# Attention and feed-forward on one core: one token layout for all pairs, per-chunk decay with the state on VectorE, and a new first block

## The chip, the cores and the metric

The kernel runs on one core of one Trainium2 chip. The metric is the device time of one execution in microseconds (us). A run is marked slow when it is over 1.5% above the fastest run of the same kernel. A "ratio" below is the recorded one of a kernel's fast runs to the fast runs of the kernel before on the same chip, with a 95% interval. It comes close to the ratio of their means, but is not exactly that, nor the ratio of the medians that stand beside it. The medians are those of all runs, slow ones too.

Engines: PE is TensorE (matmuls), PEld its weight loads, DVE is VectorE, ACT is ScalarE, POOL is GpSimd, SP is SyncE (which here only issues DMAs). "L357" is line 357 of the kernel of that run; the same statement has other line numbers in other kernels. "The Trainium skill" is a collection of notes on the chip; its pages are named by their titles.

## The reference

A linear recurrence with a decay per token (4 batches, 8 heads, 768 tokens, head size 32, state size 16), followed by a gated feed-forward layer on all 3072 tokens.

```python
# per batch and head; a in [0.85, 0.95], chunks of 32 tokens in the reference
for c in range(nc):
    cum = cumsum(log_a[chunk])
    L = exp(cum[:, None] - cum[None, :]) * causal
    y = (C @ B.T * L) @ x                         # inside the chunk
    y += (C @ state) * exp(cum)[:, None]          # from the chunks before
    state = exp(sum(log_a)) * state + sum_j exp(cum[-1] - cum[j]) * B[j] x[j]
# then, on x = y as (3072, 256), with 1536 hidden columns:
out = (maximum(x @ w_gate, 0) * (x @ w_val)) @ w_out
```

Both kernels use chunks of 128 tokens, in bf16 on TensorE. A *pair* is two chunks (256 tokens), a *block* two pairs (512 tokens); there are 12 pairs in 6 blocks. In block b, the attention of the next block's pairs P and Q is threaded between the feed-forward matmuls of block b.

## The kernel before

Pairs 0 to 3 are loaded two tokens per partition, so that a DMA packet can hold two tokens of a head instead of one. TensorE then sorts them into token order with a 0/1 matrix. Later pairs are loaded in token order.

```python
    def sort_wide(p, engs=None, own=False):
        ...
        for i in range(2):
            ...
            for r in range(2):
                nc.tensor.matmul(out=o[:, 0:128], lhsT=order[:, i, r], rhs=s["tin"][0][r], ...)
                nc.tensor.matmul(out=o[:, 128:384]..., lhsT=order[:, i, r], rhs=s["xw"][:, r], ...)
            (eng.copy if eng is nc.scalar else eng.tensor_copy)(out=bx[:, i], in_=o)
```

The decay is a running product over half a sequence. So the state needs no decay between chunks, and it grows in one PSUM bank, A_ps. VectorE only reads it through a mask.

```python
    def astep(p, i):                       # one 128x256 matmul a chunk
        nc.tensor.matmul(out=A_ps, lhsT=st[p]["B"][i], rhs=st[p]["x"][i],
                         start=(c == 0), stop=(c == NC - 2), ...)
    def sevac(p, i):                       # Sm: the state, spread for the next chunk's matmul
        nc.vector.tensor_tensor(out=n, in0=A_ps, in1=smask, op=ALU.mult)
```

The other steps of a pair: `G` computes the scores of four groups of heads into four banks, `gevac` copies them out through the causal mask (masked scores `gs`), `inter` multiplies the earlier state with C, `Dm` multiplies `gs` with x (the *masked product*), `yevac` has ScalarE move the result to `yT`, the input of the feed-forward. `gvh` and `gv` are gate and value matmuls on 256 or 512 tokens, with a relu on ScalarE and a product `h` on VectorE; `fout` is the output matmul. In the code and in the recorded texts, f counts the twelve columns of weights of 128 hidden units each. A *filler*, or warm-up matmul, is one whose result nobody uses; it only keeps TensorE busy. Five PSUM banks are shared by all steps. In the chains shown below each engine takes up its instructions in the order of the program, also where a later one could have started sooner.

```python
        if more:                            # end of a block
            inter(P, 0); inter(P, 1)
        fout(b, 0); foevac(b, 0)
        if more:
            G(P); gevac(P)
        fout(b, 1); foevac(b, 1)
        if more and b > 0:
            state(Q, 0)
        fout(b, 2); foevac(b, 2)
        if more:
            Dm(P); yevac(P, nc.scalar)
            G(Q); gevac(Q)
            state(Q, 1 if b else 0)         # behind Q's masks
        fout(b, 3); foevac(b, 3)
```

Of the kernel before, what the change touches and what calls it, by code (L numbers as in the profile page):

```python
# [29 lines left out]
def kernel(  # L30
# [18 lines left out]
    BH = NB * NH  # L49
# [5 lines left out]
    NBLK = T // 512  # L55

    const = ctx.enter_context(tc.tile_pool(name="const", bufs=1))
    glob = ctx.enter_context(tc.tile_pool(name="glob", bufs=1))
    raw = ctx.enter_context(tc.tile_pool(name="raw", bufs=4))
# [8 lines left out]




    NWIDE = 4
    st = {}

    def wide_bc(p, qb, qc):
        b, c0 = p // PPB, 2 * (p % PPB)
        sl = slice(c0 * 128, (c0 + 2) * 128)
        bcr = raw.tile([128, NH, 2, 2, N], FP32, tag="bcr", name="bcr")
        for src, j, q in ((C, 1, qc), (B, 0, qb)):
            if (p, j) in ((0, 0), (2, 1)):  # L80
                nc.vector.memset(bcr[0:1, 0, 0, 0, 0:1], 0.0)  # L81
            q.dma_start(
                out=bcr[:, :, j].rearrange("p h r n -> p h (r n)"),
                in_=src[b, :, sl, :].rearrange("h (p r) n -> p h (r n)", r=2))
        st.setdefault(p, {})["bcr"] = bcr

    def wide_x(p, *qs):

        b, c0 = p // PPB, 2 * (p % PPB)
        sl = slice(c0 * 128, (c0 + 2) * 128)  # L90
        xr = raw.tile([128, NH, 2, D], FP32, tag="xr", name="xr")
        n = NH // len(qs)
        for k, q in enumerate(qs):
            hs = slice(k * n, (k + 1) * n)
            q.dma_start(out=xr[:, hs].rearrange("p h r d -> p h (r d)"),
                        in_=x[b, hs, sl, :].rearrange("h (p r) d -> p h (r d)", r=2))
        st.setdefault(p, {})["xr"] = xr

    def load(p, qx, qb, qc):
        b, c0 = p // PPB, 2 * (p % PPB)  # L100
        if p < NWIDE:
            wide_bc(p, qb, qc)
            wide_x(p, qx)
        else:
            xr = raw.tile([128, 2, NH, D], FP32, tag="xr", name="xr")
            bcr = raw.tile([128, 2, 2, NH, N], FP32, tag="bcr", name="bcr")
            for i in range(2):
                sl = slice((c0 + i) * 128, (c0 + i + 1) * 128)
                qx.dma_start(out=xr[:, i], in_=x[b, :, sl, :].rearrange("h s d -> s h d"))
                for src, j, q in ((B, 0, qb), (C, 1, qc)):  # L110
                    q.dma_start(out=bcr[:, i, j],
                                in_=src[b, :, sl, :].rearrange("h s n -> s h n"))
            st[p] = {"xr": xr, "bcr": bcr}

    H = S // 2
    HC = NC // 2
    a_sb = glob.tile([2 * BH, H], FP32)
    nc.sync.dma_start(out=a_sb, in_=a.rearrange("b h (w s) -> (b h w) s", w=2))
    first = const.tile([1, 2], FP32)
    nc.vector.memset(first, 0.0)  # L120
    nc.scalar.activation(first[:, 1:2], first[:, 0:1], AF.Relu)


    warm = const.tile([128, 512], BF16)
    nc.vector.memset(warm, 0.0)
    wide_bc(0, nc.scalar, nc.sync)
    wide_x(0, nc.sync, nc.scalar)
    wide_bc(1, nc.scalar, nc.sync)
    wide_x(1, nc.sync)
    identf = const.tile([2 * BH, 2 * BH], FP32)  # L130
# [3 lines left out]
    maskUT = const.tile([128, 1, 128], BF16)  # L134
    make_upper_triangular(nc, maskUT[:, 0], 1.0, diag=True)
    zero1 = const.tile([2 * BH, 1], FP32)
# [3 lines left out]
    bd = const.tile([128, 128], BF16)  # L140
    nc.vector.memset(bd, 0.0)
    smask = const.tile([128, 2, 128], BF16)
    for k in range(4):
        nc.vector.memset(bd[32 * k:32 * k + 32, 32 * k:32 * k + 32], 1.0)
        nc.vector.memset(tmask[32 * k:32 * k + N, 0:1], 1.0)
    nc.vector.tensor_scalar(out=tmask[:, 1:2], in0=tmask[:, 0:1], scalar1=-1.0,
                            scalar2=1.0, op0=ALU.mult, op1=ALU.add)
    for t in range(2):
        nc.vector.tensor_scalar_mul(smask[:, t], bd, tmask[:, t:t + 1])
    pick = const.tile([2 * BH, 2, BH], FP32)  # L150
    pairs = identf.rearrange("p (h w) -> p w h", w=2)
    nc.vector.tensor_copy(pick[:, 1], pairs[:, 1])
    order = const.tile([128, 2, 2, 128], BF16)
    nc.gpsimd.memset(order, 0.0)
    for r in range(2):
        nc.gpsimd.tensor_copy(
            order[:, :, r].rearrange("p c (m r) -> p c m r", r=2)[:, :, :, r],
            ident.rearrange("p (c m) -> p c m", c=2))

    def keep_warm(n):  # L160
        w = bank("w")
        for _ in range(n):
            nc.tensor.matmul(out=w, lhsT=warm[:, 0:128], rhs=warm, start=True, stop=True)  # L163

    keep_warm(8)


# [15 lines left out]
    gate = const.tile([1, 4], FP32)  # L183

    def wait_for(p, j):

        nc.gpsimd.tensor_copy(gate[:, 2 * j:2 * j + 1], st[p]["bcr"][0:1, 0, j, 0, 0:1])

    wait_for(0, 1)
    weights(0, 4)  # L190


    cp = glob.tile([2 * BH, H], FP32)
    nc.vector.tensor_tensor_scan(
        out=cp, data0=a_sb, data1=zero1.to_broadcast([2 * BH, H]), initial=1.0,
        op0=ALU.mult, op1=ALU.add)
    rmid = const.tile([2 * BH, 1], FP32)
    nc.vector.reciprocal(rmid, cp[:, H - 1:H])
    nc.vector.tensor_scalar_mul(pick[:, 0], pairs[:, 0], rmid)

    def wide_decay(ps):

        d = bank("wdec", (128, len(ps), 2, 8))
        first = True
        for k, p in enumerate(ps):
            b, c0 = p // PPB, 2 * (p % PPB)
            for i in range(2):
                w, o = (c0 + i) // HC, ((c0 + i) % HC) * 128
                for r in range(2):
                    nc.tensor.matmul(  # L210
                        out=d[64 * i:64 * i + 64, k, r],
                        lhsT=cp[:, o + r:o + 128:2], rhs=pick[:, w, 8 * b:8 * b + 8],
                        start=first or (k == 0 and r == 0), stop=True,
                        tile_position=(0, 64 * i), skip_group_check=True)
                first = False
        return d

    def wide_factors(ps, d):
        f = const.tile([128, len(ps), 2, 2, 8], FP32, name="wf%d" % ps[0])
        nc.vector.reciprocal(f[:, :, 0], d)  # L220
        nc.vector.tensor_copy(f[:, :, 1], d)
        for k, p in enumerate(ps):
            st[p]["f"] = f[:, k].rearrange("p j r h -> p (j r) h")

    scaleBC = glob.tile([128, NB, NC, 2, 8], FP32)

    def decay():

        d = bank("dec", (128, HC, 2, NB, 8))
        for k in range(HC):  # L230
            nc.tensor.matmul(
                out=d[:, k].rearrange("p w b h -> p (w b h)"),
                lhsT=cp[:, k * 128:(k + 1) * 128],
                rhs=pick.rearrange("p w h -> p (w h)"),
                start=(k == 0), stop=True, skip_group_check=True)
        for w in range(2):
            cs = slice(w * HC, (w + 1) * HC)
            nc.vector.reciprocal(
                scaleBC[:, :, cs, 0, :].rearrange("p b k h -> p k b h"), d[:, :, w])
        for w in range(2):  # L240
            cs = slice(w * HC, (w + 1) * HC)
            nc.scalar.copy(
                out=scaleBC[:, :, cs, 1, :].rearrange("p b k h -> p k b h"), in_=d[:, :, w])

    yT = glob.tile([128, 2, T], BF16)
    A_ps = mm.tile([128, 2, 128], FP32, tag="Aps", name="A_ps")


    def scale(p, eng, ceng):
        scale_bc(p, eng)  # L250
        cast_x(p, ceng)

    def scale_bc(p, eng):
        b, c0 = p // PPB, 2 * (p % PPB)
        s = st[p]
        bs = att.tile([128, 4, 128], BF16, tag="bs", name="bs")
        if p < NWIDE:
            src = s["bcr"].rearrange("s (t q) j r n -> s (j r) t q n", t=2)
            f = s["f"]
        else:  # L260
            src = s["bcr"].rearrange("s i j (t q) n -> s (i j) t q n", t=2)
            f = scaleBC[:, b, c0:c0 + 2].rearrange("s c j h -> s (c j) h")
        for t in range(2):
            eng.tensor_tensor(  # L264
                out=bs.rearrange("s k (q t n) -> s k t q n", q=4, t=2)[:, :, t],
                in0=src[:, :, t],
                in1=f[:, :, 4 * t:4 * t + 4].to_broadcast([128, 4, 4, N]),
                op=ALU.mult)
        if p < NWIDE:
            s["tin"] = [[bs[:, 2 * j + r] for r in range(2)] for j in range(2)]  # L270
        else:
            s["tin"] = [[bs[:, 2 * i + j] for i in range(2)] for j in range(2)]
            s["B"] = s["tin"][0]
# [33 lines left out]
    def transp(p, k, apart=False):  # L307

        s = st[p]
        if "tp" not in s:  # L310
            s["tp"] = {}
# [81 lines left out]
    def astep(p, i):  # L393

        c = 2 * (p % PPB) + i
        if c == NC - 1:
            return
# [260 lines left out]
```

## Time and profile before

The median was 133.82 us. The profiled execution has a span of 132.1 us.

| what | before |
|---|---|
| first gate/value matmul | 13.56 us |
| first output matmul of block 0 | 30.44 us |
| first output matmul of block 1 | 49.84 us |
| blocks 1 to 4, from one first output matmul to the next | 18.65, 18.62, 18.51, 17.62 us |
| from block 5's first output matmul to the end | 8.8 us |

These marks are the starts of the output matmuls on the timeline of PE, where block 0's is:

```profile
30.44 1.47 PE L490 MATMUL o<-wo,h 128*128 128x256 bf16 x12
```

They cut the span at places where both kernels have done the same amount of feed-forward work, so they tell where a difference arises. (The granted-clock records start at 10.57 us at full speed in this trace, and the mean granted clock leaves out what lies before; there the warm-up matmuls of 512 columns stand 0.427 us apart, which is half speed: gate/value matmuls of 512 columns stand 0.22 us apart later.)

The page of the kernel before; in the groups the columns are line, engine, operation, output and inputs, count, then total busy us, mean ns of one, and the idle time before them with what ended it:

```profile
span 132.1 us, 3133 instructions
...
PE 125.6 (95%) x1150; PEld 83.3 (63%) x1157; DVE 90.1 (68%) x196; ACT 81.7 (62%) x177; POOL 37.6 (29%) x76
...
PEclk9999999999999999999999999999999999999999
...
PE 58%; DVE 1%; issue 0%; DVEq 0%
...
L406 DVE TENSOR_TENSOR Sm<-A_ps,smask 128x256 bf16<-128x256 f32 x20 | 8.3, 417 | 0.0
```

PE is busy 95% of the span, and in the chain of work that ended last nothing but PE counts. The other engines have room. Sm takes 417 ns.

The windows view of the kernel before, cut at the first output matmuls of blocks 1 to 5, of which one block and the sum of all four are shown (busy us of each engine, instructions in brackets, granted clock, DMA share):

```profile
core 0: us, PE busy (x) PEld busy (x) DVE busy (x) ACT busy (x) POOL busy (x), PEclk, DMA share, GB/s
...
68.49:87.11 18.62, 18.57 (x181) 12.67 (x180) 13.69 (x28) 13.04 (x29) 5.43 (x10) 1.00 0.56 85
...
sum 73.40, PE 73.11 PEld 49.76 DVE 53.28 ACT 50.31 POOL 18.29; mean PE 18.28 PEld 12.44 DVE 13.32 ACT 12.58 POOL 4.57
```

In four blocks PE is idle for only 73.40 − 73.11 = 0.29 us.

The chain of the kernel before around the two masked products of one block (start, us, what):

```profile
73.24 0.34 PE y L435 x16
73.57 0.33 PE g L361 x8
73.90 0.21 PE A_ps L398
74.12 1.31 PE o L490 x12
75.43 0.87 PE gv L478 x8
76.30 0.22 PE y L424 x4
76.52 0.34 PE y L435 x16
```

From the first masked product (L435) to the second, 3.28 us pass, all of it PE's work.

### The profile page before, as it was taken

The numbers are of one execution on the slowest core, as the hardware profiler recorded it, in microseconds if no ns is written. First come the engines' busy times: TensorE is split into PE (matmuls) and PEld (weight loads), VectorE is DVE, ScalarE is ACT, GpSimd is POOL, SyncE is SP. The second block draws the span as 40 slices with busy tenths as digits, with TensorE's granted clock in tenths as the row PEclk, the third lists the DMA queues.
The fourth block names the chain that finished last, engine by engine and source line by source line (L and its number), as shares of the span: only waits on it lengthen the run. The fifth ranks groups of instructions, "written<-read, shape, count | busy, mean of one in ns | idle before, by whom it ended". The sixth has DMA issues, their size and how long they took to land.

```text
span 132.1 us, 3133 instructions
## 1 busy us (share of the span) xinstructions
PE 125.6 (95%) x1150; PEld 83.3 (63%) x1157; DVE 90.1 (68%) x196; ACT 81.7 (62%) x177; POOL 37.6 (29%) x76
## 2 busy tenths in 40 slices
PE   6999979999999999999999999999999999999990
PEld 2455655547887457786557785467875577854770
DVE  5648867786478877569977568755879775687511
ACT  4046855393579784488774588744896935876410
POOL 7327374310266000293003390003750022100000
PEclk9999999999999999999999999999999999999999
DMA  3997999996877894239970279761110002200022
GB/s 73 189 183 111 181 210 194 183 144 83 108 136 141 95 118 47 87 86 122 106 83 5 79 137 116 90 64 58 52 57 0 0 0 84 79 0 0 5 88 71
DMA packets 68995, 12.10 MB, mean 92 GB/s; under 512 B 62772, under 2 KB 68980, under 8 KB 68980
## 3 DMA queue, kind: packets, MB, share of 16 engines
q1 hardware_dynamic: 62896, 8.88, 43.7%
q0 software_dynamic: 3184, 2.36, 11.9%
q10 hardware_dynamic: 2896, 0.66, 2.7%
q8 instruction: 9, 0.15, 0.5%
q14 instruction: 10, 0.05, 0.1%
HBM read 11.11 MB, written 3.15 MB: 108 GB/s over the span
## 4 chain that ended last, share of the span: by engine, by line
PE 58%; DVE 1%; issue 0%; DVEq 0%
PE o L490 20%; PE val L463 11%; PE gv L478 11%; PE gate L460 10%; PE y L435 2%; PE g L361 2%; PE A_ps L398 1%; PE tp L318 1%; PE y L424 1%; DVE h L467 0%; DVE ob L503 0%; DVEq L503 0%
## 5 line engine op out<-in xcount | busy, mean ns | idle before, releaser
L467 DVE TENSOR_TENSOR h<-r,val 128x512 bf16<-128x512 bf16 x48 | 32.6, 686 | 9.7 <-ACT r L466 8.8
L490 PE MATMUL o<-wo,h 128*128 128x256 bf16 x288 | 35.0, 273 | 0.1
L466 ACT ACTIVATE r<-gate 128x512 bf16<-128x512 f32 x48 | 28.3, 601 | 8.5 <-PE gate L460 6.2
L369 POOL TENSOR_SCALAR_AFFINE_SELECT gs<-gs 128x512 bf16<-128x512 bf16 (+1 forms) x24 | 12.2, 530 | 65.9 <-ACT gs L380 65.9
L490 PEld LDWEIGHTS <-h 128*128 128x128 bf16 x288 | 27.4, 98 | 5.1 <-issue 1.3
L463 PE MATMUL val<-yT,wv 128*128 128x512 bf16 x96 | 28.6, 379 | 0.3
L460 PE MATMUL gate<-yT,wg 128*128 128x512 bf16 x90 | 27.3, 379 | 0.3 <-ACT r L466 0.3
L482 DVE TENSOR_TENSOR h<-r,gv 128x256 bf16<-128x256 bf16 x48 | 19.9, 421 | 7.3 <-ACT r L481 6.9
L386 DVE TENSOR_TENSOR gs<-g,maskUT 128x512 bf16<-128x512 f32 x24 | 15.5, 686 | 13.0 <-issue 11.8
L481 ACT ACTIVATE r<-gv 128x256 bf16<-128x256 f32 x48 | 18.5, 385 | 2.5 <-PE gv L478 0.9
L478 PE MATMUL gv<-yT,wg 128*128 128x256 bf16 x96 | 18.4, 273 | 0.6 <-ACT yT L448 0.5
L478 PE MATMUL gv<-yT,wv 128*128 128x256 bf16 x96 | 18.3, 273 | 0.0
L463 PEld LDWEIGHTS <-wv 128*128 128x128 bf16 x96 | 9.4, 98 | 11.3
L460 PEld LDWEIGHTS <-wg 128*128 128x128 bf16 x96 | 8.8, 98 | 7.1 <-issue 0.5
L380 ACT CAST gs<-g 128x512 bf16<-128x512 f32 x12 | 7.1, 588 | 9.7 <-PE g L361 9.6
L448 ACT CAST yT<-y 128x512 bf16<-128x512 f32 x12 | 7.0, 586 | 8.2 <-PE y L435 7.1
L478 PEld LDWEIGHTS <-wg 128*128 128x128 bf16 x96 | 9.0, 98 | 2.4 <-issue 1.0
L478 PEld LDWEIGHTS <-wv 128*128 128x128 bf16 x96 | 9.4, 98 | 1.1
L264 POOL TENSOR_TENSOR bs<-bcr,scaleBC 128x256 bf16<-128x256 f32 x16 | 9.6, 623 | 0.0
L506 ACT COPY ob<-o 128x512 f32<-128x512 f32 x10 | 5.9, 586 | 4.7 <-PE o L490 4.7
L163 PE MATMUL w<-warm 128*128 128x512 bf16 x18 | 7.3, 556 | 1.3 <-DVE bcr L81 1.3
L406 DVE TENSOR_TENSOR Sm<-A_ps,smask 128x256 bf16<-128x256 f32 x20 | 8.3, 417 | 0.0
(75 smaller groups left out, 113.1 us busy)
## 6 DMA issues: line engine op xcount, KB each, us to landing
out_dram<-ob SPq DMA_DIRECT2D x10, 256.0 KB, 2.2
xr<-in_x_dram SPq DMA_DIRECT2D x17, 128.0 KB, 3.7
bcr<-in_B_dram SPq DMA_DIRECT2D x16, 64.0 KB, 3.6
bcr<-in_C_dram SPq DMA_DIRECT2D x16, 64.0 KB, 3.3
xr<-in_x_dram SPq DMA_DIRECT2D x3, 256.0 KB, 6.4
wg<-in_moe_w_gate_dram POOLq DMA_DIRECT2D x3, 256.0 KB, 5.0
wv<-in_moe_w_val_dram POOLq DMA_DIRECT2D x3, 256.0 KB, 6.2
wo<-in_moe_w_out_dram POOLq DMA_DIRECT2D x1, 768.0 KB, 11.3
```

The source lines that it names most:

```text
L264: eng.tensor_tensor(out=bs.rearrange("s k (q t n) -> s k t q n", q=4, t=2)[:, :, t], in0=src[:, :, t], in1=f[:, :, 4 * t:4 * t + 4].to_bro ...
L369: nc.gpsimd.affine_select(out=dst, in_=dst, pattern=[[0, n], [1, 128]], compare_op=ALU.is_ge, fill=0.0, base=0, channel_multiplier=-1)
L386: nc.vector.tensor_tensor(out=d[:, q], in0=g[q], in1=m, op=ALU.mult)
L406: nc.vector.tensor_tensor(out=n, in0=A_ps, in1=smask, op=ALU.mult)
L460: nc.tensor.matmul(out=g, lhsT=wg[:, k, fs], rhs=yT[:, k, tk], start=(k == 0), stop=(k == 1))
L463: nc.tensor.matmul(out=v, lhsT=wv[:, k, fs], rhs=yT[:, k, tk], start=(k == 0), stop=(k == 1))
L466: nc.scalar.activation(r, g, AF.Relu)
L467: nc.vector.tensor_tensor(out=fst[b][:, f], in0=r, in1=v, op=ALU.mult)
L478: nc.tensor.matmul(out=gv_[:, j], lhsT=w[:, k, fs], rhs=yT[:, k, tk], start=(k == 0), stop=(k == 1), skip_group_check=True)
L481: nc.scalar.activation(r, gv_[:, 0], AF.Relu)
L482: nc.vector.tensor_tensor(out=fst[b][:, f, u * 256:(u + 1) * 256], in0=r, in1=gv_[:, 1], op=ALU.mult)
L490: nc.tensor.matmul(out=o[:, ts % 2], lhsT=fst[b][:, f, ts * 128:(ts + 1) * 128], rhs=wo[:, f], start=(f == 0), stop=(f == NF - 1), skip_gr ...
```

## The change

The intent is to drop the sorting. All pairs are loaded two tokens per partition and used in that order. The partition of a token then no longer tells its chunk by itself: partitions 0 to 63 hold chunk 0, 64 to 127 chunk 1, with even and odd tokens side by side. So matmuls over tokens are split into tiles of 64 rows, and the mask changes. The decay is now a running product per chunk of 128 tokens. The state therefore has to be multiplied by the chunk's decay, and VectorE does that in fp32, from sums that TensorE puts into a corner of the y banks. Block 0 is written out anew. The diff, cut to its core:

```diff
-        if p < NWIDE:                       # pairs 0 to 3 wide and sorted, the others in order
-    def sort_wide(p, engs=None, own=False): ...
+    def load(p):                            # all pairs: (p r) -> p, r = 2 tokens a partition
...
-        nc.tensor.matmul(out=A_ps, lhsT=st[p]["B"][i], rhs=st[p]["x"][i], ...)
+    def adds(p, at):                        # 16 matmuls of 64x32 tiles, 64 columns
+        for r in range(2):
+            for i in range(2):
+                for q in range(4):
+                    nc.tensor.matmul(out=s["A"][i][32 * q:32 * q + 32], ...
+                        tile_position=(64 * i, 32 * q), skip_group_check=True)
...
-        nc.vector.tensor_tensor(out=n, in0=A_ps, in1=smask, op=ALU.mult)
+    def state(p):
+        for i in range(2):
+            nc.vector.scalar_tensor_tensor(out=n, in0=last["S"], scalar=decay..., in1=A, ...)
+            nc.vector.tensor_tensor(out=m, in0=n..., in1=decm..., op=ALU.mult)   # Sm
...
     def Dm(p):                              # 32 matmuls of 64x32 tiles, was 16 of 128x32
...
+    def col(p, nxt=None):
+        inter(p); Dm(p)
+        if nxt is not None: adds(nxt, p)
+        yevac(p, A_)
+        if nxt is not None: state(nxt)
...
             # end of a block
-            Dm(P); yevac(P, nc.scalar)
-            G(Q); gevac(Q)
-            state(Q, 1 if b else 0)
+            col(P, Q)                       # Q's state now ahead of Q's masks
+            G(Q); gevac(Q, (P_, V, V, V))   # one mask on POOL, three on VectorE
...
+    # block 0, before the loop
+    for f in range(4): gvh(0, f, 0)
+    pair1_a()                               # scale, cast, transpose pair 1
+    gvh(0, 4, 0); gvh(0, 5, 0)
+    pair_g(1)                               # scores, adds, masks, state of pair 1
+    gvh(0, 6, 0); gvh(0, 7, 0)
+    col(1)
+    for f in range(8): gvh(0, f, 1)
+    scan(1); factors(1); decays(1)          # decay of batches 2 and 3
...
-            nc.tensor.matmul(out=w, lhsT=warm[:, 0:128], rhs=warm, ...)          # 512 columns
+            nc.tensor.matmul(out=w[:, 0:128], lhsT=warm, rhs=warm, ...)          # 128 columns
```

## The prediction

> **What bounds it now.** TensorE: the page has PE busy 95% of 132.1 us, and the chain of waits from 50.6 us on is almost pure PE. There the blocks of 512 tokens repeat every 18.5 us, about 15.6 us of it gate/value and output matmuls, the rest attention. Other engines have room (windows: DVE 13.4, ACT 12.9, POOL 5.5 of 18.5). Before that, the first gate/value matmul starts at 13.56 us and block 0 lasts to 37.9 us, with waits, sorting matmuls and late weights (second quarter's value weights land at 19.9, output weights at 29.1).
>
> **Removed.** Sorting: 8 matmuls, about 0.65 us of PE for each of 4 pairs (timeline), about 2 us on the chain. The 128x256 state matmul (two of 0.11 us a pair) becomes 16 tiny 64-row ones. In the trace four column tiles start 3 ns apart and one round of 128 columns takes 55 ns, so with eight tiles I estimate 0.07 us: 0.15 saved a pair. Scores and masked products keep their rounds (2x110, 4x55 ns) and about 0.1 us at each change of tile mode (the Trainium skill, "TensorEngine Tiling (Array Packing)", Key Properties, says changing mode drains; the trace agrees: 0.15 and 0.20 us where a round is 0.055 and 0.11). Steady PE work falls only about 0.3 us a block. Half of the small DMA packets go, but DMA is no limit after block 0.
>
> **Added, and why it should cost more.**
> 1. State on VectorE: per chunk a 64-column and a 256-element operation, estimated 0.22 + 0.43 us (neighbours: 0.42 for 256, 0.69 for 512), against 0.42. Masks become three of 0.69.
> 2. Order. In a steady block VectorE now does the state before the next masks, and the state waits for ScalarE's eviction of y, in the same banks. ("PSUM — Partial Sum Buffer", bank collisions, says a scheduler orders even reads by two engines; no run here shows that yet.) Eviction ends 1.2 us after the masked product starts, states 0.65 to 1.3, masks 1.95: the next masked product, now 3.3 us later, would come at 3.9 to 4.5. Stall 0.6 to 1.3 us a block, plus up to 0.4 from full PSUM banks. Blocks 1 to 4: +4.5, less 1.2 saved.
> 3. Block 0, serial waits in PE's order: pair 1's transposes wait for scaling behind four h products (1.7 us); value weights 4 to 8 land near 18 to 19.5, needed at 17.7; pair 1's product waits for masks, its eviction for the state (2.5); the second decay waits for the last h, scan, 96-wide reciprocal (0.73 us in the trace) and back (3). First gate/value near 13.9, first output matmul near 34 to 35.5 (30.4 now).
> 4. Pairs 2 and 3: short slack to masks, pair 3's scaling on POOL, VectorE backlog when block 1 starts: 3 us.
>
> **Sum.** Plus 4 (block 0), 3, 3.3, some of the waits overlapping: **141.5 us**, range **135.5 to 147**. Faster by over 2%: 0.06; within 2%: 0.14; slower: 0.80.
>
> **What would show it.** PE busy share about 90%; DVE, ACT and POOL pieces in the chain in every block; blocks of 19 to 19.5 us; PE idle before masked products, released by DVE masks, and at the second decay's matmuls; DVE busy 95 to 100 us; state operations idle until the y eviction. If blocks take 18.2 us, points 1 and 2 are wrong.
>
> **What would make it wrong.** State operations much shorter than 0.65 us; the state not waiting for the eviction; weights arriving earlier because they are issued at about 4 us; the clock warming sooner than at 10.2 us. Slower still: if eight 64-row tiles do not run together, masked products and scores take twice as long (about +6 us), or a sparse startup leaves the clock cold.

## The result and the profile after

The changed kernel gives the correct result. Its median is 150.69 us (149.85 to 152.91, four runs, one of them slow), against 133.76 us before. The ratio of the fast runs is 1.128, with an interval of 1.117 to 1.139. The profiled execution is a fast one with a span of 148.2 us and a mean granted clock of 0.942.

| stretch | before | after | difference |
|---|---|---|---|
| start to block 0's first output matmul | 30.44 | 37.56 | +7.1 |
| from there to block 1's | 19.40 | 23.16 | +3.8 |
| blocks 1 to 4 | 73.40 | 78.74 | +5.3 |
| block 5's first output matmul to the end | 8.8 | 8.8 | 0.0 |
| span (rounded) | 132.1 | 148.2 | +16.1 |

The page of the changed kernel:

```profile
span 148.2 us, 4035 instructions
...
PE 127.4 (86%) x1618; PEld 88.1 (59%) x1618; DVE 97.4 (66%) x220; ACT 77.8 (53%) x168; POOL 41.8 (28%) x63
...
PEclk9965559599999999999999999999999999999999
...
PE 53%; issue 22%; DVE 11%; POOL 8%; ACT 3%; POOLq 0%; DVEq 0%
...
L357 DVE TENSOR_TENSOR Sm<-S,decm 128x256 bf16<-128x256 f32 x20 | 10.9, 545 | 0.7
...
L351 DVE SCALAR_TENSOR_TENSOR S<-S,dec,y 128x64 f32<-128x64 f32 x16 | 4.4, 275 | 7.7 <-ACT yT L397 7.7
```

PE does about as much as before in a longer span, and DVE, POOL and ACT have entered the chain. Two lines are new: the clock row holds 5s early on, and Sm, of the same size as before, now takes 545 ns on average instead of 417. The last line confirms a step of the prediction: before the state operation (S) VectorE sat idle 7.7 us in all, until ScalarE's eviction of y, which reads the same banks, was done.

The windows view of the changed kernel, blocks 2 and 3 and the sum of blocks 1 to 4:

```profile
...
80.11:100.36 20.25, 18.82 (x256) 12.97 (x255) 14.28 (x29) 12.86 (x29) 6.14 (x8) 1.00 0.37 80
100.36:121.01 20.65, 18.99 (x256) 12.97 (x255) 14.70 (x31) 12.76 (x29) 4.24 (x5) 1.00 0.08 27
...
sum 78.74, PE 75.07 PEld 51.43 DVE 55.72 ACT 49.44 POOL 18.66; mean PE 18.77 PEld 12.86 DVE 13.93 ACT 12.36 POOL 4.66
```

The clock is 1.00 here, so it has no part in these 5.3 us. PE's idle time rose from 0.29 to 3.67 us, and its busy time did not fall but rose by 2 us (a matmul whose successor waits is drawn out somewhat in the records). No other engine is near full.

The chain of the changed kernel around the two masked products of block 2, to be laid beside the chain of before:

```profile
84.77 0.35 PE y L385 x32
85.12 0.24 PE y L330 x16
...
85.38 0.60 ACT yT L397
...
86.00 0.29 DVE S L351
...
86.32 0.42 DVE Sm L357
86.74 0.20 DVE S L351
...
86.97 0.04 DVE Sm L357
87.00 0.95 issue
87.96 1.89 DVE gs L301 x3
...
89.89 0.39 PE y L385 x26
```

The second masked product now comes about 5 us after the first instead of 3.3 (so in blocks 2 and 3; in blocks 1 and 4 the distance is 3.4). Between them the chain leaves PE and walks through the y eviction (L397), two sums (L351), two Sm (L357) and three masks (L301) in single file. The 0.95 us labelled "issue" are the rest of the second Sm, which the timeline gives as 1.07 us long, from 86.97 on.

The beginning, in the windows view of the changed kernel:

```profile
10.00:15.00 5.00, 2.78 (x44) 1.80 (x43) 2.41 (x8) 0.76 (x2) 5.00 (x8) 0.50 1.00 167
...
24.00:28.00 4.00, 3.00 (x47) 2.12 (x47) 1.84 (x6) 1.34 (x3) 1.26 (x2) 0.70 1.06 185
```

The clock column (third from the right) shows half speed in this stretch. The clock records put it at 8.50 to 22.15 and at 25.56 to 28.98 us. Gate/value matmuls of 256 columns start 0.21 us apart in it, and 0.11 at full clock.

The timeline of PE in the changed kernel, where block 0's feed-forward meets the second decay; the brackets give the idle time before and what ended it:

```profile
30.57 0.38 PE L427 MATMUL gv<-yT,wv 128*128 128x256 bf16 x2
32.30 0.45 PE L193 MATMUL fac<-identf,cp 96*64 96x48 f32 x8 [1.35 <-DVE cp L184]
33.90 0.36 PE L207 MATMUL dec<-ends,heads 96*128 96x12 f32 x2 [1.15 <-DVE ends L204]
34.12 0.59 PE L410 MATMUL gate<-yT,wg 128*128 128x512 bf16 x2
...
37.56 1.47 PE L439 MATMUL o<-wo,h 128*128 128x256 bf16 x12
```

PE goes to VectorE and back twice and does almost nothing from 31.0 to 34.1 us. The last line is block 0's first output matmul. The weights were not the limit that the prediction feared: the second quarter's value weights landed at 16.96 us (18 to 19.5 predicted), before PE came to them, and the output weights at 25.95 us, 11.6 us before their use.

### The profile page after: what moved, and what is told of

Its sections match the earlier page's. It is cut to its first block, busy times and chain, and to the rows that moved or that the text cites. A ratio compares the mean times of both kernels' runs of the same rounds, so it can differ in the third digit from the quotient of the medians.

```text
span 148.2 us, 4035 instructions
## 1 busy us (share of the span) xinstructions
PE 127.4 (86%) x1618; PEld 88.1 (59%) x1618; DVE 97.4 (66%) x220; ACT 77.8 (53%) x168; POOL 41.8 (28%) x63
## 4 chain that ended last, share of the span: by engine, by line
PE 53%; issue 22%; DVE 11%; POOL 8%; ACT 3%; POOLq 0%; DVEq 0%
PE o L439 14%; PE gate L410 12%; PE val L413 12%; PE gv L427 6%; DVE gs L301 5%; POOL bs L237 3%; ACT yT L397 3%; PE w L160 2%; PE y L385 2%; DVE Sm L357 2%; POOL xb L247 1%; DVE S L351 1%; PE y L330 1%; PE g L291 1%; PE tp L260 1%
## 5 line engine op out<-in xcount | busy, mean ns | idle before, releaser
L417 DVE TENSOR_TENSOR h<-r,val 128x512 bf16<-128x512 bf16 x44 | 28.8, 685 | 11.2 <-ACT r L416 10.4
L301 POOL TENSOR_TENSOR gs<-gs,mask 128x512 bf16<-128x512 bf16 x12 | 14.1, 1171 | 77.4 <-ACT gs L310 77.4
L416 ACT ACTIVATE r<-gate 128x512 bf16<-128x512 f32 x44 | 25.6, 605 | 7.6 <-PE gate L410 6.8
L430 ACT ACTIVATE r<-gv 128x256 bf16<-128x256 f32 x56 | 21.3, 385 | 15.2 <-PE gv L427 9.1
L427 PE MATMUL gv<-yT,wg 128*128 128x256 bf16 x112 | 24.0, 300 | 5.3 <-DVE gs L301 2.4
L301 DVE TENSOR_TENSOR gs<-g,mask 128x512 bf16<-128x512 f32 x36 | 22.6, 682 | 5.7 <-PE g L291 5.7
L427 PE MATMUL gv<-yT,wv 128*128 128x256 bf16 x112 | 23.9, 299 | 0.0
L237 POOL TENSOR_TENSOR bs<-bcr,fac 128x256 bf16<-128x256 f32 (+1 forms) x22 | 14.3, 671 | 7.1 <-DMA bcr<-in_B_dram 3.9
L397 ACT CAST yT<-y 128x512 bf16<-128x512 f32 x11 | 6.4, 586 | 13.9 <-PE y L330 8.4
L357 DVE TENSOR_TENSOR Sm<-S,decm 128x256 bf16<-128x256 f32 x20 | 10.9, 545 | 0.7
L351 DVE SCALAR_TENSOR_TENSOR S<-S,dec,y 128x64 f32<-128x64 f32 x16 | 4.4, 275 | 7.7 <-ACT yT L397 7.7
```

Of the source, the lines that this page charges most:

```text
L237: eng.tensor_tensor(out=s["bs"][:, 2 * js[0]:2 * js[0] + n].rearrange("s k (q t n) -> s k t q n", q=4, t=2)[:, :, t], in0=src[:, :, t], in ...
L301: eng.tensor_tensor(out=dst, in0=src, in1=m, op=ALU.mult)
L357: nc.vector.tensor_tensor(out=m, in0=n.rearrange("s (t d) -> s t d", t=2).unsqueeze(2).to_broadcast(shape), in1=decay_of(b, c)[1].rearrang ...
L397: engs[0].copy(out=dst, in_=src)
L416: nc.scalar.activation(r, g, AF.Relu)
L417: nc.vector.tensor_tensor(out=fst[b][:, f], in0=r, in1=v, op=ALU.mult)
```

## The experiments

The changed kernel and its variants are compared by their ratio to the kernel before on their own chip. The unchanged "after" has 1.128 (1.117 to 1.139). One per cent is 1.3 us. The block marks that a recorded expectation names were read a few tenths of a microsecond later than those above where matmul records near the mark are missing; the differences between kernels do not hang on that.

| run | what was done to the changed kernel | median us | ratio (95%) |
|---|---|---|---|
| e1_warm | filler matmuls in block 0's waits | 148.37 | 1.111 (1.100 to 1.123) |
| e2c_order | state sums ahead of the y eviction, an Sm behind the masks | 147.78 | 1.100 (1.089 to 1.111) |
| e2d_no_pool_mask | Q's POOL mask given to VectorE | 150.90 | 1.135 (1.123 to 1.146) |
| e3_decay_early | second decay at the start | 147.23 | 1.108 (1.100 to 1.116) |
| e4_scale_early | pair 1 scaled ahead of block 0's products | 148.52 | 1.118 (1.110 to 1.127) |
| e5_pool_order | POOL scales pairs 3 and 4 ahead of masks | 149.75 | 1.128 (1.118 to 1.139) |
| e6_all | these together, without e2d | 139.47 | 1.042 (1.032 to 1.051) |
| e7_one_order | block 0 in the order of the other blocks | 133.89 | 1.008 (1.001 to 1.016) |
| e8_late_sum | e7 with pair 2's sums later and the output weights asked for earlier | 132.45 | 0.996 (0.991 to 1.001) |
| e9_masks_later | e8 with the odd pair's Sm later | 131.43 | 0.989 (0.983 to 0.994) |
| b1_before_warm | the kernel **before** with 128-column warm-ups | 133.50 | 1.005 (1.000 to 1.011) |

All outputs are right. The profiles of e2c, e4, e6 and e7 fell into slow runs; from those only stretches at full clock, or single instructions, are read.

### 1. Is it the cold clock? e1_warm

```diff
-    keep_warm(10)
+    keep_warm(14)
     ...
     turn(0, True)
+    keep_warm(8)
     ...
     adds(0, 0)
-    keep_warm(12)
+    keep_warm(36)
     # and 12 before yevac(0), 20 before pair1_a(), 20 before and 10 after col(1)
```

> The changed kernel with more warm-up matmuls put only where TensorE waits in block 0, nothing else moved. Theory 'clock': in the changed kernel's profile the granted clock is 0.5 from 8.5 to 22.2 us and from 25.6 to 29.0 us, and 256-column matmuls start 0.21 us apart there instead of 0.11; about 4.6 us of TensorE work is lost so. Expected: clock back to about 1.0 after 9 us, 146 us (4 to 5 us less than the changed kernel's 150.7). Rival 'waits': block 0 is set by waits on VectorE, POOL and weights alone; then the matmuls get faster but the time falls by less than 1.5 us.

The mean clock rose to 0.988, with full speed from 3.9 to 31.2 us in the profile. The ratio fell by 1.7 points, about 2.2 us; the two intervals overlap a little, and the profiled spans alone differ by 1.2 us (147.0 against 148.2). That is about half of the 4 to 5 us expected. Much of the warmth was not turned into time: at 17.0 us PE now waited 0.53 us for value weights, the wait for the second decay grew to 2.60 + 1.15 us, and behind that wait the clock fell to half once more, from 31.21 to 34.62 us. One of the three fast runs had a mean granted clock of 1.000; its span was 144.9 us, 3.3 less than 148.2, but no trace of it is kept. The cold clock is one cause, but not the main one, and part of its worth was hidden behind other waits.

### 2. The steady blocks: order or contention? e2c_order and e2d_no_pool_mask

```diff
 # e2c_order, end of a block
-            col(P, Q)
+            inter(P); Dm(P); adds(Q, P)
+            sums(Q)                          # the two S operations, ahead of the y eviction
+            yevac(P, A_)
+            masked(Q, 0)                     # first Sm
             G(Q); gevac(Q, (P_, V, V, V))
+            masked(Q, 1)                     # second Sm, behind the masks
```

> The changed kernel; in blocks 1 to 4 alone, the two sums of the state run before the eviction of y, the first product after it, the second product behind the masks. Same operations. Theory 'order': in steady blocks the masks start late since the state waits for the eviction of y and its second product is blocked by POOL's mask; expected: masked product of the next pair 3.6 to 4.0 us after that of this one instead of 3.9 to 5.2, blocks of 18.7 us instead of 19.6 to 20.7, 3.5 to 4.5 us less in all (about 146.5). Rival 'amount': VectorE simply has more to do per block (14.0 us instead of 13.3); then the order changes less than 1 us.

```diff
 # e2d_no_pool_mask, end of a block
-            gevac(Q, (P_, V, V, V))
+            gevac(Q, (V, V, V, V))
```

> The changed kernel; in blocks 1 to 4 the mask of quarter 0 of the second pair runs on VectorE (a fourth mask of 0.60 us) instead of POOL. Theory 'port': the state's product took 1.07 us instead of 0.42 twice because POOL's mask ran at the time. Expected: no product above 0.5 us in blocks 2 to 4, the two-chunk blocks (second and third of the steady four) about unchanged (0.65 won, 0.60 lost), the one-chunk blocks up to 0.6 us longer: in all 0 to 1.2 us more. Rival: the product is slow for another reason; then it stays at 1.07 us and the time grows by about 2.4 us.

The order was worth 2.8 points, about 3.7 us. The windows of e2c_order for blocks 1 to 4, all at clock 1.00, sum to:

```profile
sum 75.00, PE 74.20 PEld 51.25 DVE 55.10 ACT 49.63 POOL 18.42; mean PE 18.55 PEld 12.81 DVE 13.78 ACT 12.41 POOL 4.61
```

So 78.74 − 75.00 = 3.74 of the 5.34 us came back by reordering a few operations of VectorE and ScalarE, without touching what is computed. The masked products were 3.4 us apart in blocks 1 and 4, and 3.7 in blocks 2 and 3.

e2d was to show why an Sm takes 1.07 us. The source view of the line that makes Sm (duration min, median, max in ns), in the changed kernel and then in e2d_no_pool_mask:

```profile
L357 DVE TENSOR_TENSOR Sm<-S,decm x20: 424/426/1072, 10.8 to 127.3; 128x256 bf16<-128x256 f32 x20
```

```profile
L357 DVE TENSOR_TENSOR Sm<-S,decm x20: 424/425/674, 10.8 to 126.8; 128x256 bf16<-128x256 f32 x20
```

From block 1's first output matmul on, all of them take 424 to 426 ns once POOL masks nothing beside them (the 674 comes earlier, beside POOL's cast and scaling). In the changed kernel, an Sm that started before POOL's mask took 424 ns and the mask 1.22 us instead of 1.15; an Sm that started during the mask took 1.07 and ended 0.29 us after the mask did. The Trainium skill, "SBUF — State Buffer", section "Who interferes with whom", states this case: a VectorE operation with two inputs in SBUF and a GpSimd operation that reads SBUF exclude each other for a whole instruction, and the one that comes later is blocked. This trace agrees. Before, Sm read the state from PSUM, had one SBUF input, and never took more than 425 ns.

But e2d was not faster (1.135 against 1.128; blocks 1 to 4 took 79.82 us against 78.74, 1.1 more, as its text expected): the chain of e2d has four masks on VectorE in that place, 2.40 us, where three took 1.89, and the second Sm shortened by 0.65 us only pays for that. The contention is a real slowing of one instruction; taking it away in this manner gains nothing. Only the order helped.

### 3. Single waits of block 0: e3_decay_early, e4_scale_early, e5_pool_order

```diff
 # e3_decay_early
+    load_a(1)                                # ahead of pair 2's loads
     state(0)
+    scan(1); make_ends(1)
     yevac(0, A_, V)
+    factors(1)
     for f in range(4):
         gvh(0, f, 0)
+        if f == 1: decays(1)
-    scan(1); factors(1); decays(1)           # were behind gvh(0, 7, 1)
```

> The changed kernel with the second half of a loaded before pair 2, its scan and decay matmuls placed around the first gate/value matmuls instead of in front of the ninth f. Theory: the serial chain last h, scan, matmul, 96-wide reciprocal, second matmul cost TensorE its idle 31.0 to 34.1 us. Expected: that gap is gone, 2.5 to 3 us less (about 148). Rival: something else would have held the matmuls there anyhow (h backlog, output weights); then under 1 us.

```diff
 # e4_scale_early
+    scale(1, 1, V); scale(1, 0, P_); cast_x(1, A_)
     for f in range(4): gvh(0, f, 0)
     pair1_a()                                # without them
```

> The changed kernel with pair 1's scaling and cast issued before the first four gate/value chunks instead of behind them. Theory: TensorE waited from 16.9 to 18.25 us for VectorE's scaling, which stood behind four h products. Expected: that gap is gone, 1.0 to 1.4 us less (about 149.4). Rival 'weights': the value weights of f 4 to 7, landing at 17.0 us, would hold it instead; then under 0.5 us.

```diff
 # e5_pool_order
-    pair_g(2)
     scale(3, None, P_); cast_x(3, P_)
+    pair_g(2)
     ...
+    scale(4, None, P_); cast_x(4, P_)        # was in the loop
     pair_g(3)
```

> The changed kernel with POOL's scaling and casts of pairs 3 and 4 ahead of the masks of pairs 2 and 3, not behind them. Theory: TensorE waits 0.43 us for pair 4's cast, and the state's products run at the same time as POOL's scaling (0.55 to 0.67 us instead of 0.42). Expected: products of pairs 2 and 3 at 0.42 us, 0.5 to 1.0 us less. Rival: masks and evictions alone set the pace; then no change.

With the decay early the gap at 31 to 34 us is gone, block 0's first output matmul comes at 34.65 instead of 37.56 us, and the ratio falls by 2.0 points, about 2.7 us. Scaling pair 1 early closes the gap at 16.9 to 18.3 us and brings 1.0 point, about 1.3 us (the intervals overlap; that the wait is gone is seen in the profile). The POOL order is a miss: the wait for POOL's cast (0.43 us) went, but the next wait, for the y eviction, grew from 0.74 to 1.1 us, and the time is the same. The other half of its theory was not tested: the Sm of these pairs still ran beside POOL's scaling and took 0.55 to 0.64 us, not the 0.42 expected.

### 4. Do the causes add up? e6_all

The edits of e1 (without the fillers before the first y eviction and before pair 1), e2c, e3, e4 and e5 in one kernel.

> The changed kernel with all five edits: warm-up matmuls (2.3 us gained alone), early second decay (2.7), the state's sums before the eviction in steady blocks (3.7), early scaling of pair 1 (about 1.2), POOL order (about 0.7). If the causes add up: 139 to 141 us. If they overlap (a wait taken away uncovers the next one): 142 to 145. In both cases still slower than the kernel before, as the steady blocks keep about 0.3 us each and block 0 its serial masks.

Separately they had given 2.2 + 3.7 + 2.7 + 1.3 + 0 = 9.9 us by their ratios. Together the ratio fell by 8.6 points, 11.5 us (the two fast runs took 138.05 and 138.41 us, a little less than the 139 to 141 expected). The intervals are too wide to tell 9.9 from 11.5, but the gains did not shrink when they were put together: these waits follow each other in PE's queue. If the joint gain is larger, that is what e1 would lead one to expect, as part of the clock's worth was hidden behind waits that are gone here. What held e6 back then is seen on its timeline of PE:

```profile
15.10 0.38 PE L448 MATMUL gv<-yT,wg 128*128 128x256 bf16 x2
16.99 0.39 PE L448 MATMUL gv<-yT,wv 128*128 128x256 bf16 x2 [1.51 <-DMA wv<-in_moe_w_val_dram]
```

The early start ran into the value weights. From block 0's first output matmul to block 1's it still took 24.65 us; this profile is a slow run with half clock from 45.45 to 48.86, and at full clock the same stretch took 23.16 in the changed kernel. Block 0's written-out order was the remaining suspect.

### 5. Were the operations or the order to blame? e7_one_order, e8_late_sum, e9_masks_later

e7 keeps the design of the changed kernel (layout, 64-row tiles, masks, sums, state on VectorE) and changes the order of block 0. It goes through the same loop as the other blocks, pair 1 is scaled on POOL and transposed during the first masks, and the order at the end of a block is that of e2c; the second decay is computed during block 0's gate/value matmuls. With this some work changes its engine or size: pair 1's C is scaled on POOL too, the transposes of pairs 1 to 3 are moved by ScalarE alone, block 0 uses 512-token gate/value matmuls for eight of its twelve columns of weights as the other blocks do, and the fillers are those of e1 in part.

```diff
-    for f in range(4): gvh(0, f, 0)
-    pair1_a()
-    ...                                      # all of block 0, and pairs 2 and 3
-    for b in range(1, NBLK):
+    scale(1, None, P_)                       # behind cast_x(0)
+    weights(4, 8)                            # ahead of POOL's first mask
+    turn(1); tevac(1, A_, A_); cast_x(1, A_) # behind the first masks
+    col_g(0, 1)                              # pair 0's product, pair 1's sums and scores
+    for b in range(NBLK):
```

> The changed kernel's operations in a new order: block 0 runs like the other blocks (pair 1 scaled and transposed during the first masks, its scores before the first gate/value matmul; pairs 2 and 3 masked behind two output chunks), second-quarter weights issued ahead of POOL's first mask, the sums of the state before the eviction of y everywhere, warm-up matmuls in TensorE's early waits. Theory 'order': the 64-row design is not slow in itself, its loss is the order of VectorE, ScalarE and POOL; then the stretch from the first output matmul to that of block 1 falls from 24.7 us (in the kernel with five edits) to about 19 to 20, the first output matmul comes at 26 to 28 us, and the time is 130 to 134 us, level with the kernel before. Rival 'design': the extra work on VectorE and the serial state keep it at 136 us or more whatever the order.

The time fell to 133.89 us, 0.8% above the kernel before. Block 0's first output matmul to block 1's took 19.53 us, against 23.16 in the changed kernel, both at full clock (the 24.65 of e6 holds half clock). The first output matmul itself came at 32.03 us, not at 26 to 28. The profile, a slow run, names the next wait on the timeline of PE:

```profile
15.62 0.42 PE L406 MATMUL y<-gs,xb 64*32 64x128 bf16 x32
18.89 0.31 PE L338 MATMUL y<-xb,bs 64*32 64x64 bf16 x16 [2.85 <-POOL xb L255]
```

Pair 2's sums (L338) came too early for pair 2's x, which lands at 18.17 us; the wait of 2.85 us was followed by half clock from 17.93 to 24.76. (Four of the five fast runs had a granted clock of 1.000, so the half clock is this slow run's; whether the fast ones had the same wait, no trace shows.) e8 moves those sums behind pair 2's scores and asks for the output weights before POOL's cast of pair 2:

```diff
     col_g(0, 1)
+    weights_out(0, NF)
     cast_x(2, P_)
-    weights_out(0, NF)
     ...
-                col(W, P if more else None)
+                col(W, P if more and b else None)
         ...
             G(P)
+            if b == 0:
+                adds(P, P); state(P)
```

> The kernel in one order, with two edits: pair 2's state matmuls move from pair 1's column behind pair 2's scores, and the output weights are asked for before POOL's cast of pair 2. In that kernel's profile TensorE waited 2.85 + 0.72 us at 16 to 19.9 us for the cast of pair 2, whose x landed at 18.2 us behind the weights, and then ran at half clock to 24.8 us. Expected: no wait there, clock full, first output matmul at 27 to 29 us (32.0), 129.5 to 131.5 us, faster than both kernels. If the output weights (landed 27.8) become the new wait: 131 to 133.

The median is 132.45 us, level with the kernel before (0.991 to 1.001) and above the 129.5 to 131.5 expected; the output weights were not the new wait, as they landed at 25.37 us. The clock is full from 5.82 us on, and block 0's first output matmul comes at 27.19 us (before: 30.44). What was left in the steady blocks is shown by the chain of e8_late_sum:

```profile
55.84 0.24 PE y L338 x16
...
56.10 0.59 ACT yT L418
...
56.72 0.24 DVE S L358
...
56.98 0.42 DVE Sm L373
57.41 0.20 DVE S L360
...
57.63 0.42 DVE Sm L373
58.06 0.34 DVE h L452
...
58.44 0.60 PE gv L448 x4
```

The two Sm stand ahead of the product h, for which PE waits, though nothing needs them before the block's end. e9 moves them behind the fifth and seventh gate/value of the block:

```diff
         yevac(p, A_)
-            state(nxt)
+            sums(nxt)
         ...
         for f in range(4, NF):
             gv(b, f)
+            if more and b and f in (4, 6):
+                masked(P, (f - 4) // 2)
```

> e8 with one reordering in blocks 1 to 4: after the odd pair's y eviction VectorE does the two state sums of the next pair and then the gate/value products; the two masked products of 0.42 us each follow after the fifth and the seventh gate/value of the block, since the inter-chunk matmuls that read them come only at the block's end. In e8 the chain of waits ran there through the sums and the masked products (0.24, 0.42, 0.20, 0.42, then the gate/value product) before TensorE could go on. My theory, that the order of VectorE's instructions and not the new operations costs the time: about 0.3 to 0.5 us less a block, 1 to 2 us in all, so 130.5 to 131.5 us and 0.980 to 0.992 of the kernel before. The rival, that in e8 TensorE has enough other work queued to hide these stalls: within 0.3% of e8, about 132.4 us. Correct result in either case.

The same place in the chain of e9_masks_later:

```profile
54.82 0.16 PE y L338 x16
54.98 2.73 PE gv L448 x24
```

PE no longer leaves. The median is 131.43 us, and the ratio 0.989 (0.983 to 0.994): the design that took 150.69 us is 1.1% faster than the kernel before, by an interval that excludes 1, though within the 2% that count as the same. The windows of e9_masks_later for blocks 1 to 4 sum to:

```profile
sum 74.21, PE 73.89 PEld 51.26 DVE 55.51 ACT 50.01 POOL 18.66; mean PE 18.47 PEld 12.81 DVE 13.88 ACT 12.50 POOL 4.67
```

So the steady blocks still take 0.8 us more than before (73.40). What e9 wins lies in front of them: block 0's first output matmul comes at 27.09 us instead of 30.44. In sum, what the change cost came back by order, by a few moves between engines, and by fillers, without a change of the design. That the design is worth the 1.1% is not shown: the kernel before was not given the same care, such as an earlier issue of the second quarter's weights (landed at 14.79 us in e9, at 19.88 before).

### 6. Does the kernel before owe its start to the clock? b1_before_warm

```diff
 # the kernel before
-    warm = const.tile([128, 512], BF16)
+    warm = const.tile([128, 128], BF16)
-    keep_warm(8)      # then 4, then 7, of 512 columns
+    keep_warm(34)     # then 14, then 30, of 128 columns
```

> The kernel before with denser warm-up: 128-column warm-up matmuls as in the changed kernel (34, 14 and 30 instead of 8, 4 and 7 of 512 columns), nothing else. In its profile the clock was half until 10.6 us. If the early start is set by TensorE at half clock: clock full by 7.5 us and 0.5 to 1.5 us less than before. Rival: the start is set by loads and VectorE; then within 0.3 us.

The clock was full from 4.99 us in the profile instead of 10.57, and the time did not fall (1.000 to 1.011). In the profile the first gate/value matmul came earlier, at 12.15 instead of 13.56 us, and block 0's first output matmul at 29.72 instead of 30.44. But the fast runs of the kernel before lie in two groups, 132.0 to 132.7 and 133.1 to 133.9 us, whose cause is open, and its profile is one of the upper group; two profiles cannot settle 0.7 us here. By the runs, the earlier clock brought no gain. That e8 and e9 beat the old start does not come from the shorter fillers alone: their first gate/value matmul is later (14.10 and 14.00 us), and yet they reach the output matmul at 27.19 and 27.09, against 29.72.

## Why the prediction was wrong

The direction held, and most of the mechanisms; the size did not. Against the time before, the prediction had +7.7 us, and the fast profiles show +16.1. Its sum was "plus 4 (block 0), 3, 3.3, some of the waits overlapping". Of what is missing, about 3.1 us lie in block 0, 2.6 in the discount for overlap, 2.0 in blocks 1 to 4 and 0.8 in pairs 2 and 3.

- **The step that failed: "some of the waits overlapping".** The terms summed to 10.3 us, and 2.6 were taken off. Between the terms nothing overlapped: each of the three shows up in full, and more, in its own stretch of the table (7.1, 3.8 and 5.3 us), and the gains of the single edits did not shrink in e6_all. The waits stand at different times in PE's queue, and PE has hardly any spare time in the steady blocks (0.29 us idle in four of them before). Only inside block 0 did one cause hide behind another, as e1 shows.
- **"Plus 4 (block 0)": +7.1.** The first gate/value matmul was predicted at 13.9 us and came at 13.35. The waits that point 3 lists come to 1.7 + 2.5 + 3 = 7.2 us, but the sum took only 4 for the block. On PE's timeline they were 1.33 (pair 1's scaling), 1.42 + 0.74 (pair 1's product and eviction) and 1.35 + 1.15 us (the second decay), 6.0 in all. The feared wait for value weights did not come. And the clock was left out of the sum: "a sparse startup leaves the clock cold" stood under what would make it slower still, and it happened. The Trainium skill, "TensorE: Matmul & The Clock Gate", Part 1, says that half speed is the default and that a window of about 3.4 us decides; the records here come in pieces of 3.41 us and multiples of it, and agree. By e1 the cold clock is worth 1.2 (profiles) to 2.2 us (ratios) while other waits cover part of it. The waits themselves were named rightly: the second decay was put at 3 us, e3 gained 2.7; pair 1's scaling was put at 1.7, e4 gained 1.3.
- **Pairs 2 and 3, "3 us": +3.8.** Nearly right. e5 shows that the wait for POOL's cast was not what set it; Sm beside POOL's scaling was not taken away there, so that part is untested. e7 shows that another order brings the stretch back to 19.53 us. Which single wait in it cost most stays open.
- **Blocks 1 to 4, "+4.5, less 1.2 saved": +5.3.** The stall was sized well: e2c took back 3.74 us, and e9's move of Sm took another 0.80 (from 75.01 in e8 to 74.21), 4.5 in all. The saving was not there: 74.21 us is still 0.8 more than before, where 1.2 less was forecast. In the steady blocks the sixteen small matmuls of 64 columns, which follow a masked product, start 8 to 9 ns apart, not 3 to 4, and take 0.24 us a pair, not the estimated 0.07; two of the old ones took 0.11 us each. (Where they follow the scores instead, as in block 0, they do start 3 to 4 ns apart; why is open.) With scores and masked products added, the starts of PE in e9 give 6.7 us in blocks 1 to 4 against 6.6 before (the time from each such matmul to the next). That 64-row tiles run eight at a time is true (in a masked product groups of eight start within 0.03 us, the later groups 0.055 us apart); that this would save time on PE in these blocks is not.
- **"The state waits for ScalarE's eviction of y": right,** 7.7 us in six waits. The Trainium skill, "PSUM — Partial Sum Buffer", section "PSUM bank collisions raise a hardware error", says that the compiler's scheduler orders any two engines on one bank and quadrant, reads too. The trace agrees: in the chain shown, S starts 0.03 us after the eviction ends, and in e2c, where S comes first, the eviction waits for S.
- **"State operations 0.22 + 0.43": right when alone** (0.28 and 0.42), except where POOL works beside Sm (1.07). That contention was not foreseen. Taking it away in e2d did not make the kernel faster.
- The marks named to test it spoke clearly: PE at 86% (predicted about 90), VectorE at 97.4 us (95 to 100), blocks of 19.4, 20.3, 20.7 and 18.5 us (19 to 19.5), and VectorE, ACT and POOL in the chain.

## What to carry to other kernels

When one engine is near full, waits that stand at different places of its queue add up, as they did here, and a discount for overlap needs a reason; cut the span at marks of equal work and add the differences. Removing work from the bottleneck engine is worth little if the replacement, on an idle engine, is put in single file ahead of what the bottleneck waits for next: put operations whose results are needed late behind those that are needed soon. Before a new design is given up as slow, its operations are worth running in the order of the old one: here the same design took 150.7 us in one order and 131.4 us in another.

## What the Trainium skill lacked or had wrong

- "TensorE: Matmul & The Clock Gate", Part 3, "Measured speedup vs the span model", gives about 4 ns for each further tile. The trace agrees for matmuls of 128 columns (3 to 4 ns), but 16 matmuls of 64-row tiles with 64 columns started 8 to 9 ns apart where they followed a masked product (blocks 1 to 4), and 3 to 4 ns apart, in groups of eight, where they followed the scores (block 0). No page has this case.
- The same page, Part 1, puts the cost of the clock ramp at under 1% of a typical kernel. Here it was not the first ramp alone: after it a sparse start brought half speed back for 13.65 + 3.41 us, and e1_warm gained 1.7 points in the ratio.
- The same page says that an idle window of about 3.4 us throttles and a busy one releases, but not how busy a window must be. In the changed kernel the clock fell at 8.50 us after a window in which PE was busy for 0.61 of the time, mostly with small matmuls, while the windows from 28.98 and from 32.39 us, with 0.60 and 0.66, were followed by full speed. The threshold stays open.
- "SBUF — State Buffer", "Who interferes with whom", was right here (424 ns alone, 1070 when begun during POOL's mask). That section lacks the time from the release to the end of the blocked operation, 0.29 us for Sm's 128x256 elements here; elsewhere the page has such a time for another pair only.
- "PSUM — Partial Sum Buffer" and "TensorEngine Tiling (Array Packing)" agreed where they were used; a change of tile mode cost about 0.1 us (gaps of 0.15 and 0.20 us between matmuls that are otherwise 0.05 and 0.11 apart).
